# Four edits and a new instruction order in a fused attention, gMLP and expert-attention kernel: a twin copy from PSUM, a normalisation in one product, a minimum as a reduction

## The chip, the core and the metric

The kernel runs on one core of a Trainium2 chip. The metric is the device time of one execution in microseconds (us), as the median over several runs. The engines named below are PE (TensorE, which multiplies matrices), PEld (its weight loads), DVE (VectorE), ACT (ScalarE), POOL (GpSimd) and SP (SyncE, which issues the transfers between HBM and the on-chip memory). SBUF is the on-chip memory. PSUM is the eight banks into which PE writes its results.

## The reference

Three layers follow each other. The inputs are fp32.

```
# 1: attention with a window of 64; 4 batches, 8 heads, 576 positions, head size 64
scores = scale * q @ k^T;  mask: 0 <= i - j < 64
attn = softmax(scores);    x = attn @ v           -> x: (4, 576, 512)
# 2: gated MLP
h = relu(x @ w_in);  u, v = h[:, :512], h[:, 512:]
v_n = (v - mean(v)) / sqrt(var(v) + 1e-6)
x = (u * (w_spatial @ v_n + b_spatial)) @ w_out   -> x: (4, 576, 512)
# 3: four experts, two of them per token, each a causal attention
logits = x @ w_gate;  the two largest per token -> weights w (softmax over the two)
for e in 4 experts:
    q, k, v = x @ wq[e], x @ wk[e], x @ wv[e]
    a = softmax(causal(scale * q @ k^T))
    out += w[:, e] * (a @ v @ wo[e])
```

The products of the second and third layer are computed from fp32 numbers that are split into a high part and a low part, so that most products appear as two or three matmuls.

## The kernel before

A small list scheduler, the class Planner, lays out the program when the kernel is built. Each step is a node with the engines that may run it and a cost on each, the nodes that it waits for, the buffers that it uses, and a priority. The planner goes through the ready nodes, takes for each engine the one that stands best, and writes out the instructions in that order. Nothing of it runs on the chip: what the chip sees is one fixed instruction list for each engine, and semaphores between them. Three dictionaries named SHIFT (one for PE steps, one for the other engines, one for transfers) add a number to the priority of each single node. A few scalars weigh the rest: SWITCH (a change between kinds of matmul), DVE_BIAS and POOL_BIAS (which engine takes a step that several could run), EFT and others. So a new table means a new order on every engine, and a step that may run on several engines may land on another one.

The planner runs twice. The first run holds the first attention (function a_couple), the unpacking of the weights (prep64, lines 674 to 696), and the first product of the gMLP with its statistics and the spatial mix. The second run holds the rest: the projections q and k of the third layer (c_qk), v (c_v, c_vt), the gate (c_gate), the causal attention in units of a row block and an expert (unit), the product with v (c_pv), with wo (c_wo), and the splitting of the layer's input into high and low part (c_split, names xh and xl).

The steps that matter here, by their lines:

- The start. `heat` issues WARM filler matmuls at the very start and FILL = 60 more where PE would have nothing to do. They multiply the identity by itself (L333, `bank<-ident`).
- First attention, in steps of three 128x128 blocks. PE forms the scores (names vt, ut, kt for k and qa for q). DVE adds the mask and takes the row minimum (L546). ACT takes the exponential (L552). DVE sums and inverts (L568, L570). `s_norm` scales the three blocks, each with its own column of factors, on ACT (L558) or on DVE or POOL (L560). PE transposes the result (L564), and it is multiplied by v (`pt,woh`).
- Projection k (c_qk). The product lies in a PSUM bank. `hi` rounds it into kd, one half of the partitions for each of two experts. `lo` subtracts that from the bank (its result is named kz in the trace, L357). `twin` puts a second copy of the high part into the other half of the partitions of kd. In the kernel before it copies kd to kd within SBUF, and waits for `hi`.
- The gate (c_gate, L1155 to L1170) is a chain of some fifteen small DVE instructions, ranks the four logits and leaves the weights in fx.
- A unit: PE forms the scores from kd, kz and qs. DVE adds the causal mask and takes the minimum (L1207). For the last block of rows there are two halves, and L1216 takes the smaller of the two minima. ACT takes the exponential (L1219). DVE adds a small number to the sum and inverts it (L1221, L1222). DVE or POOL scales by the inverse and by fx (L1223), so that this step waits for the gate. PE transposes (L1239), the result is copied to pg, and PE multiplies pg by v (`pg,v`).

Of the kernel before, what the change touches and what calls it, by code (L numbers as in the profile page):

```python
# [26 lines left out]
SWITCH = 107920.0  # L27
A_BIAS = 10098.0
C_BIAS = 162315.0
DVE_BIAS = (1136.0, 1147.0)  # L30
POOL_BIAS = (1131.0, 1068.0)
WARM = 8
FILL = 60
LOADS = (-130000, -120000, -43801, -5807, 14591, 18276, 34028)
EFT = (636.0, 778.0)
# [233 lines left out]
def attn_gmlp_moe_kernel(ctx: ExitStack, tc: tile.TileContext, kq0, qT, kT, v, w_in, wspT, b_sp, w_outT,  # L269
# [6 lines left out]
    HS = S // 2  # L276
# [221 lines left out]
    def a_couple(n0):  # L498
# [25 lines left out]
        def vap(x, vi, e):  # L524
            b, p, _ = grp[x]
            c = e * 64 + (0 if b else (p % 2) * 128)
            return hv[x][:, vi, c:c + 64]

        def s_mm(_):
            for j in range(3):  # L530
                for x, e in ((0, 0), (1, 1), (1, 0), (0, 1)):
                    win = max(0, 64 * (3 * grp[x][2] + j - 1))
                    mm(bank[e][HALF[x], j * 128:(j + 1) * 128], qap(x, j, e), kap(x, win, e))

        def mask(j):
            return MASK[tuple(int(3 * g + j > 0) for _, _, g in grp)]

        S_N[n0] = S_N[n0 + 1] = top = N((PE, 816), s_mm, kn + [Q_N[n0], Q_N[n0 + 1], S_N.get(n0 - 1)], alloc=bank, use=hk, prio=prio,
                                        form=1)
        done = []  # L540
        for ps, pt in zip(bank, pts):
            pa, mx, ps2 = r_pa.new(), r_mx.new(), r_at.new()

            def s_top(_, ps=ps, pa=pa, mx=mx):
                for j in range(3):
                    dve.tensor_tensor_reduce(out=pa[:, j, :], in0=ps[:, j * 128:(j + 1) * 128],  # L546
                                             in1=mask(j), scale=-0.125, scalar=3.0e38,
                                             op0=ALU.add, op1=ALU.min, accum_out=mx[:, j, 0:1])

            def s_exp(_, pa=pa, mx=mx):  # L550
# [4 lines left out]
            def s_norm(e, pa=pa, mx=mx):  # L555
                for j in range(3):
                    if e == ACT:
                        act.activation(pa[:, j, :], pa[:, j, :], AF.Copy, scale=mx[:, j, 3:4])  # L558
                    else:
                        engs[e].tensor_scalar(pa[:, j, :], pa[:, j, :], mx[:, j, 3:4], 1.0, op0=ALU.mult, op1=ALU.mult)  # L560
# [460 lines left out]
    def c_qk(b, pr, h, nm):  # L1021
# [28 lines left out]
        else:  # L1050
# [9 lines left out]

            def twin(e):
                for x in range(2):
                    copy(e, kd[x][HALF[1 - x], tk], kd[x][HALF[x], tk])
            n1 = N(halves(HS), hi, [a], use=[ps] + kl + kd)
            n2 = N((DVE, 2 * t_tt(HS) + 185), lo, [n1], use=[ps] + kl + kd)
            n3 = N(halves(HS, False), twin, [n1], use=kd, sbuf=True)
            a = N({DVE: 0.0}, lambda e: None, [n2, n3])
        QK_N.setdefault((b, pr, nm), []).append(a)

    V2, V2_N, LG_N, FX = {}, {}, {}, {}  # L1070
    VT, VT_N = {}, {}

# [356 lines left out]
```

## Time and profile before

| quantity | value |
|---|---|
| median of 3 runs | 450.18 us (449.14 to 451.76) |
| the profiled execution, its own time | 450.96 us |
| its span, first to last instruction | 449.2 us |
| PE busy | 439.7 us, 98% of the span |
| PEld busy | 397.4 us, 88% |
| DVE busy | 315.9 us, 70% |
| ACT busy | 293.7 us, 65% |
| POOL busy | 105.5 us, 23% |
| chain that ended last, PE's share | 80% (DVE 8%, ACT 6%, DMA 3%) |
| mean granted TensorE clock | 0.996 |

1.76 us of the profiled execution's time lie outside the span. The busy shares are means over stages that differ. The profile gives for any stretch of the span the busy time of each engine, the TensorE clock that was granted (1.00 is 2.4 GHz, half of it 1.2 GHz) and the share of time in which the transfer engines worked. For each engine it gives what ended its idle times. A group of instructions is shown as line, engine, operation and `output<-input`, with the minimum, median and maximum of its durations in ns. Matmul durations overlap, since matmuls are pipelined.

### The profile page before, as it was taken

To read this page: it belongs to the slowest core of one execution; us is meant where nothing else is said; L and a number is where in the kernel's file an instruction comes from. 1 tells how busy PE (TensorE), PEld (TensorE's weight loads), DVE (VectorE), ACT (ScalarE), POOL (GpSimd) and SP (SyncE) were. 2 spreads that over 40 slices of the span, in tenths; PEclk is the share of its full clock that TensorE was granted. 3 is DMA by queue.
4 is the path that set the end of the run, shared out by engine and by line. 5 is a ranking of instruction groups with operands and counts; after the bars stand their busy time and mean duration, and the time that the engine had idled before them with its cause. 6 is when DMAs were issued, how large, how long until landed. Compare 5 with 4: busy or idle time off the path is not lost.

```text
span 449.2 us, 10878 instructions
## 1 busy us (share of the span) xinstructions
PE 439.7 (98%) x3962; PEld 397.4 (88%) x3962; DVE 315.9 (70%) x1291; ACT 293.7 (65%) x926; POOL 105.5 (23%) x168
## 2 busy tenths in 40 slices
PE   8999999999999999999999999899999999999996
PEld 7887899989899879999899999699899979897875
DVE  4999989962866989024535547988697987787650
ACT  4989989562766968213422347887585978777863
POOL 4335763300300225000100341710031011012110
PEclk9999999999999999999999999989999999999999
DMA  8993737040242505003001000000010001000114
GB/s 286 302 312 113 249 109 233 19 139 0 63 148 65 174 4 140 0 1 95 1 1 48 1 0 2 0 2 3 0 48 26 0 2 49 0 1 25 72 50 161
DMA packets 31079, 33.10 MB, mean 74 GB/s; under 512 B 1905, under 2 KB 24689, under 8 KB 31026
## 3 DMA queue, kind: packets, MB, share of 16 engines
q1 hardware_dynamic: 31026, 32.41, 23.1%
q8 instruction: 31, 0.51, 0.5%
q14 instruction: 22, 0.18, 0.1%
HBM read 27.68 MB, written 4.72 MB: 72 GB/s over the span
## 4 chain that ended last, share of the span: by engine, by line
PE 80%; DVE 8%; ACT 6%; DMA 3%; issue 2%; POOL 2%; POOLq 0%; ACTq 0%
PE bank L333 72%; PE bank L1239 5%; DMA y<-in_w_in_dram 3%; PE bank L564 3%; ACT pa L552 1%; DVE p L1207 1%; ACT pa L558 1%; DVE p L1223 1%; ACT p L1219 1%; DVE qs L357 1%; POOL p L1223 1%; DVE xh L348 1%; ACT bank L679 0%; ACT pt L344 0%; DVE kz L357 0%
## 5 line engine op out<-in xcount | busy, mean ns | idle before, releaser
L333 PE MATMUL bank<-xh,w 128*128 128x288 f32 x512 | 109.6, 298 | 0.0
L333 PEld LDWEIGHTS bank<-xh,w 128*128 128x128 f32 x512 | 84.1, 188 | 0.9 <-DVE st L767 0.2
L333 PE MATMUL bank<-xl,w 128*128 128x288 f32 x256 | 75.3, 294 | 0.0
L333 PE MATMUL bank<-w,xh 128*128 128x512 f32 (+1 forms) x256 | 65.1, 344 | 0.0
L552 ACT ACTIVATE pa<-pa,mx 128x128 f32<-128x128 f32 x144 | 55.8, 398 | 5.5 <-DVE mx L546 5.4
L333 PEld LDWEIGHTS bank<-xl,w 128*128 128x128 f32 x256 | 48.2, 188 | 0.4
L333 PEld LDWEIGHTS bank<-w,xh 128*128 128x128 f32 x256 | 43.5, 190 | 5.4 <-ACT pt L344 0.2
L1219 ACT ACTIVATE p<-p,mc 128x128 f32<-128x128 f32 (+4 forms) x72 | 41.8, 582 | 8.6 <-DVE mc L1207 7.1
L1223 POOL TENSOR_SCALAR p<-p,mc,fx 128x256 f32<-128x256 f32 (+4 forms) x26 | 17.1, 661 | 113.9 <-DVE mc L1222 54.8
L333 PE MATMUL bank<-w,xl 128*128 128x512 f32 (+1 forms) x128 | 43.4, 339 | 0.0
L333 PE MATMUL bank<-wsp_h,vh 128*128 128x288 f32 x128 | 38.6, 302 | 0.0
L333 PE MATMUL bank<-wsp_h,vl 128*128 128x288 f32 x128 | 37.7, 295 | 0.0
L333 PE MATMUL bank<-wsp_l,vh 128*128 128x288 f32 x128 | 37.7, 294 | 0.0
L1207 DVE CUSTOM_DVE_ANT_0 p<-bank,cmask 128x128 f32<-128x128 f32 (+4 forms) x72 | 33.2, 482 | 6.1 <-PE bank L333 4.2
L770 POOL TENSOR_TENSOR st<-st,nhalf 128x1 f32<-128x1 f32 (+1 forms) x20 | 11.5, 573 | 98.3 <-DVE st L769 98.3
L1239 PE MATMUL bank<-ident,p 128*128 128x128 f32 x192 | 30.8, 282 | 2.9 <-DVE mc L1221 1.9
L344 ACT ACTIVATE pg<-bank 128x128 f32<-128x128 f32 (+4 forms) x71 | 29.2, 440 | 6.6 <-PE bank L1239 6.0
L546 DVE CUSTOM_DVE_ANT_0 pa<-bank,mask 128x128 f32<-128x128 f32 x120 | 28.3, 284 | 5.2 <-POOL mx L415 4.1
L333 PE MATMUL bank<-kd,qs 128*128 128x128 f32 (+5 forms) x96 | 30.9, 338 | 0.0
L1239 PEld LDWEIGHTS bank<-ident,p 128*128 128x128 f32 x192 | 23.2, 143 | 7.4 <-DVE mc L1221 2.9
L333 PE MATMUL bank<-kz,qs 128*128 128x128 f32 (+5 forms) x96 | 28.7, 316 | 0.0
L552 ACT ACTIVATION_READ_ACCUMULATOR pa<-pa,mx 128x1 f32 x144 | 28.4, 197 | 0.0
(209 smaller groups left out, 1077.0 us busy)
## 6 DMA issues: line engine op xcount, KB each, us to landing
vt<-in_v_dram SPq DMA_DIRECT2D x12, 512.0 KB, 4.5
qa<-in_qT_dram SPq DMA_DIRECT2D x44, 96.0 KB, 3.8
out_dram<-ot SPq DMA_DIRECT2D x15, 256.0 KB, 2.0
y<-in_w_in_dram SPq DMA_DIRECT2D x7, 512.0 KB, 7.2
kt<-in_kT_dram SPq DMA_DIRECT2D x12, 288.0 KB, 4.4
y<-in_w_outT_dram SPq DMA_DIRECT2D x4, 512.0 KB, 4.3
y<-in_wspT_dram SPq DMA_DIRECT2D x2, 576.0 KB, 4.0
vt<-in_kq_dram SPq DMA_DIRECT2D x2, 384.0 KB, 3.8
```

The lines of the kernel that those rows point to most:

```text
L333: pe.matmul(o, lhsT, rhs, start=start, stop=stop)
L344: act.activation(o, i, AF.Copy)
L348: engs[e].tensor_copy(o, i)
L357: engs[e].tensor_tensor(out=o, in0=a, in1=hi.bitcast(F32), op=ALU.subtract)
L546: dve.tensor_tensor_reduce(out=pa[:, j, :], in0=ps[:, j * 128:(j + 1) * 128], in1=mask(j), scale=-0.125, scalar=3.0e38, op0=ALU.add, op1=A ...
L552: act.activation(pa[:, j, :], pa[:, j, :], AF.Exp, bias=mx[:, j, 0:1], scale=-1.0, accum_out=mx[:, j, 1:2])
L564: pe.transpose(ps2[:, j * 128:(j + 1) * 128], pa[:, j, :], ident)
L770: a = N((POOL, 464), lambda e: pool.tensor_tensor(out=st[:m, 9:10], in0=st[:m, 8:9], in1=nhalf[:m], op=ALU.pow), [n1], use=[st])
L1207: dve.tensor_tensor_reduce(out=P[:, a0:a1], in0=ps[:, :w], in1=msk, scale=-0.125, scalar=3.0e38, op0=ALU.add, op1=ALU.min, accum_out=mc[:, ...
L1219: a = N((ACT, 284 + 0.87 * L), lambda e: act.activation(P[:m, :L], P[:m, :L], AF.Exp, bias=mc[:m, 0:1], scale=-1.0, accum_out=mc[:m, 2:3]) ...
L1223: a = N({POOL: 328 + 0.832 * L, DVE: 90 + 0.52 * L}, lambda e: engs[e].tensor_scalar(P[:, :L], P[:, :L], mc[:, 3:4], fx[:, I, ev:ev + 1], ...
L1239: pe.transpose(ps[:, j * m:(j + 1) * m], P[:, j * 128:(j + 1) * 128], ident)
```

## The change

The edits by themselves are small; the three tables and the scalars above replace the whole order.

```
-SWITCH = 107920.0
+SWITCH = 76763.0
-DVE_BIAS = (1136.0, 1147.0)
-POOL_BIAS = (1131.0, 1068.0)
-WARM = 8
+DVE_BIAS = (1180.0, 1793.0)
+POOL_BIAS = (1364.0, 1322.0)
+WARM = 4
-EFT = (636.0, 778.0)
+EFT = (759.0, 1125.0)
 SHIFT = (
...
-        S_N[n0] = S_N[n0 + 1] = top = N((PE, 816), s_mm, kn + [Q_N[n0], Q_N[n0 + 1], S_N.get(n0 - 1)], alloc=bank, use=hk, prio=prio,
+        S_N[n0] = S_N[n0 + 1] = top = N((PE, 816 if n0 else 1500), s_mm, kn + [Q_N[n0], Q_N[n0 + 1], S_N.get(n0 - 1)], alloc=bank, use=hk, prio=prio,
...
             def s_norm(e, pa=pa, mx=mx):
-                for j in range(3):
-                    if e == ACT:
+                if e == ACT:
+                    for j in range(3):
                         act.activation(pa[:, j, :], pa[:, j, :], AF.Copy, scale=mx[:, j, 3:4])
-                    else:
-                        engs[e].tensor_scalar(pa[:, j, :], pa[:, j, :], mx[:, j, 3:4], 1.0, op0=ALU.mult, op1=ALU.mult)
+                else:
+                    engs[e].tensor_tensor(out=pa.t, in0=pa.t, in1=mx[:, :, 3:4].to_broadcast([128, 3, 128]), op=ALU.mult)
...
             def twin(e):
                 for x in range(2):
-                    copy(e, kd[x][HALF[1 - x], tk], kd[x][HALF[x], tk])
+                    copy(e, kd[x][HALF[1 - x], tk], ps[HALF[x], :HS])
...
-            n3 = N(halves(HS, False), twin, [n1], use=kd, sbuf=True)
+            n3 = N(halves(HS), twin, [a], use=[ps] + kl + kd)
...
-        def N_(c, f, deps, alloc=()):
-            return N((DVE, c), lambda e: f(), deps, alloc=alloc, use=[] if alloc else [ex, ga, gb])
+        def N_(c, f, deps, alloc=(), sbuf=True):
+            return N((DVE, c), lambda e: f(), deps, alloc=alloc, use=[] if alloc else [ex, ga, gb], sbuf=sbuf)
...
-            tops = [N((DVE, 70), lambda e: dve.tensor_tensor(out=mc[:m, 0:1], in0=mc[:m, 0:1], in1=mc[:m, 1:2],
-                                                             op=ALU.min), tops, use=[mc], prio=prio)]
+            tops = [N((DVE, 75), lambda e: dve.tensor_reduce(out=mc[:m, 0:1], in_=mc[:m, 0:2], axis=AX.X, op=ALU.min),
+                      tops, use=[mc], prio=prio)]
```

The cost numbers in the nodes (816, 1500, 70, 75 and the like) are the planner's weights, and change only the order. The flag `sbuf` of the gate's steps is such a weight too. Of the gate's instructions none changes.

The PE list goes from 2237 to 2231 rows, the DVE list from 1210 to 1224, ACT from 522 to 516, SP from 74 to 77; POOL keeps 139. Nearly every row of the PE list stands elsewhere. Three places show how.

The first is the head of SP's list, the transfers of the first stage. in_v is read into woh and wol, in_kT into ut and kt, in_qT into qa. Before:

```order
L426 DMA vt<-in_kq_dram 128x768 x2
L426 DMA w_149<-in_w_in_dram 128x1024
L426 DMA woh<-in_v_dram 128x2x256
L426 DMA y_152<-in_w_in_dram 128x1024
L426 DMA y_154<-in_w_in_dram 128x1024
L426 DMA y_156<-in_w_in_dram 128x1024
L426 DMA wol<-in_v_dram 128x2x256
L426 DMA qa<-in_qT_dram 128x192 x2
L426 DMA ut<-in_kT_dram 128x4x256
```

After:

```order
L426 DMA vt<-in_kq_dram 128x768 x2
L426 DMA woh<-in_v_dram 128x2x256
L426 DMA wol<-in_v_dram 128x2x256
L426 DMA w_147<-in_w_in_dram 128x1024
L426 DMA ut<-in_kT_dram 128x4x256
L426 DMA qa<-in_qT_dram 128x192 x2
L426 DMA y_166<-in_w_in_dram 128x1024
L426 DMA ut<-in_kT_dram 128x4x192
L426 DMA y_169<-in_w_in_dram 128x1024
L426 DMA y_178<-in_w_in_dram 128x1024
```

The first piece of k (ut) moves ahead of three of the four pieces of w_in.

The second is DVE where the third layer's attention begins. L1207 is the mask and minimum of a unit, L1221 and L1222 its sum and inverse, L1155 to L1170 the gate, `lg_104` the logits of the first batch. Before, the gate's last rows stand ahead of the first units:

```order
L1169 TENSOR_TENSOR fx<-fx,gb 128x20
L1170 COPY fx<-fx 64x2
L357 TENSOR_TENSOR kz_3625<-bank_70,kd 64x288
L357 TENSOR_TENSOR kz_3626<-bank_70,kd 64x288
L1207 ISA p,mc<-bank_69,cmask 128x128
L1207 ISA mc 128x1
L1207 ISA p,mc<-bank_66,cmask 128x256
L1207 ISA mc 128x1
L1207 ISA p,mc<-bank_71,cmask 128x128
```

After:

```order
L1207 ISA p,mc<-bank_66,cmask 128x256
L1207 ISA mc 128x1
L1221 TENSOR_SCALAR mc<-mc 128x1
L1087 COPY lg_104<-bank_69 128x4
L1222 RECIPROCAL mc<-mc 128x1
L1155 TENSOR_REDUCE gb<-lg_104 128x5
L1221 TENSOR_SCALAR mc<-mc 128x1
L1156 TENSOR_TENSOR ga<-lg_104 128x80
L1222 RECIPROCAL mc<-mc 128x1
```

The whole first gate moves from ahead of the first four units' L1207 to behind them, and the first L1223 of these units stands behind L1170. The third is DVE a little ahead of that place, where the k projections of the first batch are finished. In the kernel before DVE has only the rows `kz` there, and both copies of kd are ACT's. After:

```order
L348 CAST kd<-bank_69 64x288 x2
L357 TENSOR_TENSOR kz_3555<-bank_69,kd 64x288
L357 TENSOR_TENSOR kz_3556<-bank_69,kd 64x288
L357 TENSOR_TENSOR kz_3557<-bank_67,kd 64x288
L357 TENSOR_TENSOR kz_3558<-bank_67,kd 64x288
L1087 COPY lg_104<-bank_68 128x4
L348 CAST kd<-bank_72 64x288 x2
```

A pair `CAST kd<-bank` is a twin that now runs on DVE. 12 of the 16 twins do so after, none before; the other 4 stay on ACT. In the program after, each of the 12 still waits for ACT as well as for PE.

## Rows read from the trace of the kernel before

**Rows 1.** Windows: us, PE, PEld, DVE, ACT, POOL busy (instructions), PEclk, DMA share, GB/s

```profile
6.00:46.00 40.00, 38.62 (x502) 33.23 (x498) 36.61 (x176) 36.42 (x140) 16.99 (x28) 1.00 0.83 264
46.00:280.00 234.00, 234.00 (x2267) 218.08 (x2260) 151.09 (x595) 131.78 (x439) 55.63 (x85) 1.00 0.23 70
...
289.00:293.00 4.00, 2.12 (x17) 1.98 (x16) 4.00 (x14) 1.92 (x5) 1.86 (x2) 0.95 0.00 0
293.00:297.00 4.00, 4.00 (x24) 3.95 (x24) 2.36 (x15) 3.05 (x10) 0.77 (x1) 0.62 0.00 0
...
300.00:446.00 146.00, 144.84 (x1058) 125.67 (x1056) 108.40 (x436) 108.17 (x303) 19.59 (x25) 1.00 0.09 31
```

**Rows 2.** Waits of PE: line, waited for: us in total, times, longest

```profile
PE bank L1239 <- DVE mc L1221: 1.9, 1, 1.9
...
PE bank L1239 <- POOL p L1223: 0.7, 3, 0.3
PE bank L564 <- DVE pa L560: 0.7, 1, 0.7
...
PE bank L1239 <- DVE p L1223: 0.2, 1, 0.2
```

**Rows 3.** Chain that ended last, a piece of it: start, us, what

```profile
30.84 5.00 DMA y<-in_w_in_dram
```

**Rows 4.** Fillers, by form: duration ns minimum/median/maximum, first and last start

```profile
L333 PE MATMUL bank<-ident x136: 272/275/579, 1.6 to 203.0; 128*128 128x128 f32 x136
```

**Rows 5.** s_norm and subtractions with two SBUF operands, by form, same columns

```profile
L560 DVE TENSOR_SCALAR pa<-pa,mx x75: 270/282/1474, 10.6 to 177.6; 128x128 f32<-128x128 f32 x75
...
L357 DVE TENSOR_TENSOR vl<-vr,vh x10: 692/693/695, 99.7 to 224.0; 128x512 fp32r<-128x512 f32 x10
...
L357 DVE TENSOR_TENSOR xl<-pa,xh x5: 459/459/461, 235.1 to 257.6; 128x288 fp32r<-128x288 f32 x5
```

**Rows 6.** Timeline at 22 to 26 us, DVE and POOL: start, us, engine, line

```profile
23.18 1.53 DVE L560 TENSOR_SCALAR pa<-pa,mx 128x128 f32<-128x128 f32 x3
25.16 0.67 DVE L560 TENSOR_SCALAR pa<-pa,mx 128x128 f32<-128x128 f32 x3
...
22.97 1.27 POOL L357 TENSOR_TENSOR w<-y,w 128x512 fp32r<-128x512 f32 x1 [2.82 <-ACT w L344]
```

**Rows 7.** Timeline, 288 to 292 us, DVE, POOL, ACT and PE

```profile
288.09 2.77 POOL L357 TENSOR_TENSOR xl<-y,xh 128x576 fp32r<-128x576 f32 x2
...
288.24 1.27 DVE L1216 TENSOR_TENSOR mc<-mc 128x1 f32<-128x1 f32 x1
...
289.44 1.64 DVE L1223 TENSOR_SCALAR p<-p,mc,fx 128x384 f32<-128x384 f32 x1
289.61 0.78 ACT L1219 ACTIVATE p<-p,mc 128x576 f32<-128x576 f32 x1 [0.66 <-DVE mc L1216]
...
291.14 0.55 PE L1239 MATMUL bank<-ident,p 128*128 128x128 f32 x3 [1.88 <-DVE mc L1221]
```

**Rows 8.** The minimum of two halves, L1216, by form

```profile
L1216 DVE TENSOR_TENSOR mc<-mc x8: 148/158/1274, 288.2 to 420.5; 128x1 f32<-128x1 f32 x8
```

**Rows 9.** Copies of k's high part, by form

```profile
L344 ACT ACTIVATE kd<-kd x32: 428/442/446, 264.7 to 416.2; 64x288 fp32r<-64x288 f32 x32
...
L344 ACT ACTIVATE kd<-bank x30: 388/406/408, 264.0 to 415.4; 64x288 fp32r<-64x288 f32 x30
L348 DVE CAST kd<-bank x2: 450/455/460, 301.0 to 301.5; 64x288 fp32r<-64x288 f32 x2
```

**Rows 10.** First and last instruction of a gate, from DVE's timeline

```profile
309.04 0.18 DVE L1155 TENSOR_REDUCE gb<-lg 128x5 f32<-128x20 f32 x1
...
312.33 0.17 DVE L1170 COPY fx<-fx 64x2 f32<-64x2 f32 x1
```

**Rows 11.** The mask of a unit and its exponential, by form

```profile
L1207 DVE CUSTOM_DVE_ANT_0 p<-bank,cmask x72: 273/452/692, 279.9 to 429.6; 128x128 f32<-128x128 f32 x16, 128x256 f32<-128x256 f32 x16, 128x384 f32<-128x384 f32 x16, 128x512 f32<-128x512 f32 x16
...
L1219 ACT ACTIVATE p<-p,mc x72: 387/604/779, 280.3 to 431.3; 128x128 f32<-128x128 f32 x16, 128x256 f32<-128x256 f32 x16, 128x384 f32<-128x384 f32 x16, 128x512 f32<-128x512 f32 x16
```

More of the change, by code (lines that the diff above doesn't have):

```diff
@@ L570, in a_couple @@
             a = N((DVE, 91), lambda e, mx=mx: dve.reciprocal(mx[:, :, 3], mx[:, :, 3]), [a], use=[mx], prio=prio)
-            a = N({POOL: 1053, DVE: 450, ACT: 880}, s_norm, [a], use=[pa, mx], prio=prio, sbuf=True)
+            a = N({POOL: 955, DVE: 468, ACT: 880}, s_norm, [a], use=[pa, mx], prio=prio, sbuf=True)
             a = N((PE, 327), p_t, [a], alloc=[ps2, pt], use=[pa], prio=prio)
@@ L1149, in lead @@
             return m1(n)[:, :, None].to_broadcast(s3)
-        def N_(c, f, deps, alloc=()):
-            return N((DVE, c), lambda e: f(), deps, alloc=alloc, use=[] if alloc else [ex, ga, gb])
+        def N_(c, f, deps, alloc=(), sbuf=True):
+            return N((DVE, c), lambda e: f(), deps, alloc=alloc, use=[] if alloc else [ex, ga, gb], sbuf=sbuf)
         tt, tr_ = dve.tensor_tensor, dve.tensor_reduce
-        n1 = N_(90, lambda: tr_(out=m1(0), in_=lg, axis=AX.X, op=ALU.max), LG_N[b], [ex, ga, gb])
+        n1 = N_(90, lambda: tr_(out=m1(0), in_=lg, axis=AX.X, op=ALU.max), LG_N[b], [ex, ga, gb], False)
         n2 = N_(155, lambda: tt(out=gt(), in0=lf, in1=le, op=ALU.is_gt), [n1])
@@ L1160, in c_gate @@
         n4 = N((ACT, 210), lambda e: act.activation(ex.t, ex.t, AF.Exp), [n4], use=[ex])
-        nf = N_(0, lambda: None, [n2, n3, n4])
+        nf = N_(0, lambda: None, [n2, n3, n4], sbuf=False)
         n2 = N_(155, lambda: tt(out=gt(), in0=gt(), in1=eq(), op=ALU.add), [n2, n3])
-        n2 = N_(150, lambda: tr_(out=rk(), in_=gt(), axis=AX.X, op=ALU.add), [n2])
+        n2 = N_(150, lambda: tr_(out=rk(), in_=gt(), axis=AX.X, op=ALU.add), [n2], sbuf=False)
         n2 = N_(80, lambda: dve.tensor_scalar(rk(), rk(), 1.5, None, op0=ALU.is_lt), [n2])
         n2 = N_(90, lambda: tt(out=ex.t, in0=ex.t, in1=rk(), op=ALU.mult), [n2, n4])
-        n2 = N_(90, lambda: tr_(out=m1(1), in_=ex.t, axis=AX.X, op=ALU.add), [n2])
+        n2 = N_(90, lambda: tr_(out=m1(1), in_=ex.t, axis=AX.X, op=ALU.add), [n2], sbuf=False)
         n2 = N_(70, lambda: dve.tensor_scalar(m1(1), m1(1), 1e-9, None, op0=ALU.add), [n2])
-        n2 = N_(75, lambda: dve.reciprocal(m1(1), m1(1)), [n2])
+        n2 = N_(75, lambda: dve.reciprocal(m1(1), m1(1)), [n2], sbuf=False)
         n4 = N_(90, lambda: tt(out=ex.t, in0=ex.t, in1=lead(1), op=ALU.mult), [n2])
```

6 rows, old and new, of the table SHIFT are left out of this document.

## The prediction, made before the changed kernel was timed

> **What bounds the kernel now.** I read the stretches of the span first, then what PE waited for, then the timeline at the one long wait. The windows [rows 1] show four stages with different limits. From 6 to 46 us PE is busy for 38.62 of 40 us, but 64 of the 68 fillers (136 instructions) lie before 44 us and give the next stage nothing [rows 4]. DVE is busy for 36.61 us there and ACT for 36.42: the first stage is set by the chain mask, exponential, sum, scaling, and by DVE above all. From 46 to 280 us PE is busy for 234.00 of 234.00 us. There a shorter step on another engine buys nothing, and only a new hole in PE can cost. From 280 to about 297 us the attention of the third layer starts, and PE has its only long hole: 1.88 us, all of it behind one DVE instruction [rows 2, 7]. Right behind it the granted clock falls to a mean of 0.95 in 289 to 293 us and 0.62 in 293 to 297 us [rows 1], that is, to its lower level for a few microseconds. From 300 us to the end of the matmuls PE is busy for 144.84 of 146 us, with DVE at 108.40 and ACT at 108.17, about 74% each. Its waits there are short, all on the scaling L1223: 0.7 us in three places and 0.2 us in one, 0.2 us each [rows 2].
>
> So what can be won is small: fillers and holes ahead of 46 us, the 1.88 us with the clock behind it, and some 1 us later on. What can be lost is open on the other side, since the order is new throughout.
>
> **Yardstick.** The profiled execution took 450.96 us, 0.78 above the median of 450.18. Each term below is a difference to that execution, and the sum is taken off the median, as the terms don't depend on the 0.78. 0.5% is 2.25 us, about what a measurement of this kernel can tell from no change; faster begins at 447.93, slower at 452.43.
>
> **Edit 1, the product in s_norm.** Three scalings on DVE take 0.67 us as a group where nothing disturbs, and 1.53 us where POOL runs a subtraction of two SBUF operands beside it [rows 6]. One product over 384 columns lies between 0.46 us (288 columns) and 0.69 us (512 columns) [rows 5], by a straight line 0.56 us: 0.11 us less a group. There were 25 such groups (75 instructions), and some ten ahead of 46 us, so about 1.1 us less for DVE in the stage that it sets, from 0 to 2 by the ends. The groups behind 46 us lie beside a full PE and give nothing. POOL's seven groups I cost at nothing for the same reason; were one late, PE would wait for its transposes, as it did once for DVE, 0.7 us [rows 2].
>
> The 1.53 us stand beside a POOL subtraction, and the 0.67 us two microseconds later do not [rows 6]. The Trainium skill, "SBUF — State Buffer", § Who interferes with whom, says of this that scalings which use both ports and products with two SBUF operands alike share a port with POOL, one of the two blocking for a whole instruction. By that rule the one product loses as much to POOL as the three scalings, and the sum keeps 0.11 us a group and not more; the rows of the scalings agree, and no row here shows a product beside POOL.
>
> **Edit 2, L1216.** The minimum of two columns took 0.15 us mostly and 1.27 us once, beside POOL's two subtractions of 2.77 us [rows 7, 8]. The exponential behind it began 0.66 us late. The next DVE instruction, an L1223, was stretched to 1.64 us by the same neighbour, and L1221 came behind that: that queue is the 1.88 us of PE. As a reduction over one operand, the step lies between 0.15 us (L1216 undisturbed) and 0.18 us (L1155, the gate's reduction) [rows 8, 10] if POOL does not hold it, and at 1.27 us if it does. I take 0.18. Alone this would free about 1.1 us of the 1.88, as the stretched L1223 stays what it is. The 1.27 us row lies wholly within POOL's 2.77 us. The same page of the Trainium skill says that on this chip a reduction never blocks against POOL, so by it the step stays short wherever the new order puts it; no row here shows a reduction of mc beside POOL.
>
> **Edit 3, the twin.** A copy from SBUF takes ACT 442 ns, from PSUM 406 ns, and DVE from PSUM 455 ns [rows 9]. It would start without waiting for `hi`, but the program after makes each of the 12 twins on DVE wait for ACT too, which reads the same bank. So what was 0.81 us (hi, two copies) and then 0.92 us of `lo` on DVE beside 0.88 us of twin on ACT, 1.7 us, becomes 0.81, 0.91 and 0.92 one behind the other, 2.6 us. That is 0.9 us later for 12 of 16 steps, hidden where k is ready well ahead of its scores. And DVE gets 12 x 0.91 = 10.9 us more to do and ACT 12 x 0.88 = 10.6 us less, most of it behind 300 us, where DVE goes from 74% to about 81%. I take it into the last term below.
>
> **The order, stage by stage.** *To 46 us.* WARM 8 to 4 takes four fillers off; at the start the clock is low and they stand ahead of nothing that is late, so this is worth nothing by itself to some 0.9 us if PE's queue is what is late. k's first piece moves ahead of three pieces of w_in. In the kernel before, the chain ran through w_in's transfers, 5.00 us in one piece [rows 3], so w_in later can cost, and k earlier can help. Laying the DVE work out in either order up to the same first-attention step gives nearly the same amount before (32 us) and after, less the 1.1 us of edit 1. I take a gain of **1.3 us**, range -0.7 to 2.2.
>
> *46 to 280 us.* PE is full; in the new order at least 5.5 us of PE work lie between a score product and its transposes (at least 6.1 before). **0**, down to -0.5.
>
> *280 to 297 us.* Before: 1.88 us of hole, 0.27 us of small ones and some 0.5 us of smaller lateness, 2.7 us; and the clock, (1 - 0.62) x 4 + (1 - 0.95) x 4 = 1.7 us [rows 1]. Together 4.4. After: the gate stands behind the first four L1207, and the first L1223 behind the gate. A gate took 3.5 us from first to last instruction [rows 10], of which 1.1 us went to other work between; so 2.4 us. With four masks (1.5 us) and eight small instructions of 0.15 us, 5.3 us pass on DVE between the first mask and the first scaling, and 0.34 us of scaling (128 columns, the least of L1223) follow. PE has ten units of scores in a row and a projection behind them, 4.9 us, ahead of the first transpose. So PE waits there about 0.8 us, then 0.4 us for the copy ahead of `pg,v`, and 0.2 to 1.1 us where the v products want their split input: 2.3 us, range 1.2 to 3.5. No single hole reaches 1.88 us, and I expect the clock to stay. Gain 4.4 - 2.3 = **2.1 us**, range 0.9 to 3.2.
>
> *300 us to the end.* I laid the matmuls of either order end to end at the durations of their groups and read how much PE work lies between a unit's last score product and its first transpose. The unit needs L1207 (0.45 us), L1219 (0.60) with its sum, L1221, L1222 and L1223, with hand-overs 2.2 to 3.4 us [rows 11]. Before, 4 units of 80 had under 2.8 us, and four waits of 0.2 us stand in the trace [rows 2]. After, 11 units have under 2.8, four of them in one burst. 7 more x 0.2 = **1.4 us lost**, range from a gain of 0.5 to a loss of 3.0, the upper end if DVE's added 10.9 us fall on these units. The last matmul and the output transfer stay as they are.
>
> Sum: 1.3 + 0 + 2.1 - 1.4 = 2.0 us less. 450.18 - 2.0 = **448.2 us**.
>
> **Rivals.**
> 1. *The last term does not appear.* ACT is relieved by 10.6 us and L1216 is no longer stretched, so the short units get their exponential sooner. For it: ACT was as busy as DVE. Against it: DVE takes what ACT loses. The gate may also be hidden. Time: 448.2 - 1.4 - 1.2 = 445.6. Chance 0.20.
> 2. *The gate is late enough to bring the clock down again.* The holes at 280 us add up in one place, as with the 1.88 us before. For it: it fell once, behind one such hole [rows 1, 7]. Against: mine are spread over three places. Time: 448.2 + 1.7 = 449.9. Chance 0.17.
> 3. *The start gives nothing*, because w_in's later transfer holds DVE as it did [rows 3]. Time: 448.2 + 1.3 = 449.5. Chance 0.12.
> 4. *The change does not do what it says of the twin*: k is later by 0.9 us. Were 4 of the 12 not hidden, 3.6 us: 448.2 + 3.6 = 451.8. Against: before, PE shows no wait for kd or kz. Chance 0.05.
> 5. *Slower.* DVE becomes the bound behind 300 us: twins, a gate and masks queue ahead of a scaling, PE has a hole of the kind at 289 us, and the clock falls again: 1.88 + 1.7 = 3.6 us each. One such hole with rival 2 gives 450.18 - 1.3 - 0.4 + 1.4 + 3.6 = 453.5. It decides from a DVE queue of about 2 us more than the unit's cover. Chance 0.10.
>
> **How the numbers follow.** The forecast has 0.36, with its own range of 446.2 to 450.3 by the terms' ends. A little under half of it is faster by over 0.5%. Faster: 0.45 x 0.36 + 0.20 + a little of 2 and 3 = 0.40. Slower: rival 5, half of 4, and the forecast's tail: 0.15. Same: 0.45. The range reaches from rival 1 to just past the start of slower, 445.0 to 452.2, leaving out most of rival 5 and the faster half of a better rival 1.
>
> **What would show it.** The first product over kt should end its wait 1 to 1.5 us sooner (edit 1 and the start). No hole over 1.5 us at 280 to 297 us, and the clock at 1.00 there; if the clock falls, rival 2. L1216 never over 0.3 us. DVE about 81% busy behind 300 us, with some ten waits of 0.2 us on L1223; fewer speak for rival 1, one of 2 us for rival 5. A wait of PE for kd or kz would show rival 4. The prediction is wrong if PE is no longer full between 46 and 280 us, or if one of the new waits lies where nothing of before showed one.

## Result and profile after the change

The changed kernel took 453.51 us in the median of five runs (452.73 to 454.01), against 450.18 before: 1.0067 times as long, 95% interval 1.0045 to 1.0089. The forecast was 448.2, in a range of 445.0 to 452.2, so it was wrong in size and in sign. The profiled execution took 452.73 us, 1.77 more than the profiled one of before, with a span of 450.9 us and a granted clock of 1.00 throughout. The other four executions had means of 0.995 to 0.999. The profiled one of before had paid 1.7 us for its clock, so like for like the distance is about 3.5 us, against 3.3 us by the medians.

The windows after, with the columns of [rows 1]:

```profile
6.00:46.00 40.00, 39.22 (x508) 33.97 (x506) 37.13 (x166) 36.09 (x136) 17.52 (x24) 1.00 0.84 270
46.00:280.00 234.00, 233.59 (x2239) 217.39 (x2240) 150.45 (x572) 133.30 (x433) 51.15 (x70) 1.00 0.23 69
280.00:289.00 9.00, 7.42 (x54) 6.17 (x53) 7.94 (x41) 6.08 (x20) 4.96 (x6) 1.00 0.00 1
...
293.00:297.00 4.00, 3.27 (x26) 2.91 (x26) 3.32 (x15) 2.62 (x10) 0.77 (x1) 1.00 0.02 4
...
300.00:446.00 146.00, 142.30 (x1037) 122.48 (x1036) 109.55 (x444) 101.76 (x291) 20.23 (x26) 1.00 0.08 28
```

PE stays full from 46 to 280 us but for 0.41 us, the end of a hole that began at 45.7 us. Its idle time from 300 to 446 us went from 1.16 [rows 1] to 3.70 us. Of the 1.16 us of before, 0.36 lie behind the last matmul, so the stretch behind 300 us lost some 2.9 us. The waits of PE after, as in [rows 2]:

```profile
PE bank L1239 <- POOL p L1223: 1.9, 3, 1.1
...
PE bank L1239 <- DVE p L1223: 1.1, 3, 0.7
PE bank L333 <- ACT pg L344: 0.7, 1, 0.7
...
PE bank L1239 <- DVE lg L1087: 0.6, 1, 0.6
PE bank L1239 <- DVE mc L1221: 0.6, 1, 0.6
PE bank L1239 <- DVE pg L348: 0.5, 1, 0.5
```

The one hole of 1.9 us is gone, and many of 0.5 to 1.1 us have come. In none of them does PE wait for kd or kz. DVE's own waits tell more. First the kernel before, then the changed one:

```profile
DVE kz L357 <- ACT kd L344: 4.8, 3, 2.1
```

```profile
DVE kd L348 <- ACT kd L344: 13.2, 11, 2.2
...
DVE kz L357 <- ACT kd L344: 1.1, 2, 0.6
```

DVE stood still for ACT's first copy of k for 4.8 us in 3 places before, and for 14.3 us in 13 places after. Here is what that does at the longest hole, from the timeline of the changed kernel:

```profile
298.15 0.19 ACT L1219 ACTIVATION_READ_ACCUMULATOR p<-p,mc 128x1 f32 x1
...
298.24 0.81 ACT L344 ACTIVATE kd<-bank 64x288 fp32r<-64x288 f32 x2
...
299.09 0.92 DVE L348 CAST kd<-bank 64x288 fp32r<-64x288 f32 x2 [0.77 <-ACT kd L344]
...
299.94 0.14 DVE L1221 TENSOR_SCALAR mc<-mc 128x1 f32<-128x1 f32 x1
300.11 0.92 DVE L357 TENSOR_TENSOR kz<-bank,kd 64x288 fp32r<-64x288 f32 x2
301.06 0.16 DVE L1087 COPY lg<-bank 128x4 f32<-128x4 f32 x1
301.26 0.17 DVE L1222 RECIPROCAL mc<-mc 128x1 f32<-128x1 f32 x1
...
301.59 0.55 POOL L1223 TENSOR_SCALAR p<-p,mc,fx 128x256 f32<-128x256 f32 x1 [2.62 <-DVE mc L1222]
...
302.20 0.44 PE L1239 MATMUL bank<-ident,p 128*128 128x128 f32 x2 [1.07 <-POOL p L1223]
```

The twin waits 0.77 us for ACT and takes 0.92, kz takes 0.92 behind it, and the reciprocal of a unit whose sum of exponentials was there at 298.34 us stands in DVE's queue behind both, at 301.26. POOL waits for that, and PE for POOL: 1.07 us.

### The profile page after: what moved, and what is told of

Same layout as the page of the kernel before. It is cut to its first block, busy times and chain, and to the rows that moved or that the text cites. A ratio compares the mean times of both kernels' runs of the same rounds, so it can differ in the third digit from the quotient of the medians.

```text
span 450.9 us, 10833 instructions
## 1 busy us (share of the span) xinstructions
PE 438.6 (97%) x3954; PEld 394.6 (88%) x3954; DVE 315.9 (70%) x1264; ACT 289.1 (64%) x908; POOL 102.0 (23%) x149
## 4 chain that ended last, share of the span: by engine, by line
PE 80%; DVE 9%; ACT 7%; issue 1%; POOL 1%; ACTq 0%; POOLq 0%; DVEq 0%
PE bank L333 73%; PE bank L1239 4%; PE bank L564 3%; ACT p L1219 2%; DVE p L1207 2%; ACT pa L552 1%; DVE kz L357 1%; DVE kd L348 1%; ACT kd L344 1%; ACT xh L344 1%; ACT pg L344 1%; DVE xl L357 1%; DVE p L1223 1%; DVE pa L546 1%; ACT pt L344 0%
## 5 line engine op out<-in xcount | busy, mean ns | idle before, releaser
L1223 POOL TENSOR_SCALAR p<-p,mc,fx 128x256 f32<-128x256 f32 (+4 forms) x27 | 18.7, 692 | 129.5 <-ACT p L1219 34.1
L1207 DVE CUSTOM_DVE_ANT_0 p<-bank,cmask 128x128 f32<-128x128 f32 (+3 forms) x72 | 33.3, 483 | 5.4 <-PE bank L333 4.4
L344 ACT ACTIVATE pg<-bank 128x512 f32<-128x512 f32 (+4 forms) x79 | 31.9, 435 | 3.1 <-PE bank L1239 2.3
L1239 PEld LDWEIGHTS bank<-ident,p 128*128 128x128 f32 x192 | 22.1, 140 | 10.5 <-POOL p L1223 4.1
L333 PE MATMUL bank<-kd,qs 128*128 128x288 f32 (+5 forms) x96 | 30.1, 330 | 0.0
L344 ACT ACTIVATE pt<-bank 128x384 f32<-128x384 f32 x42 | 19.0, 491 | 15.9 <-PE bank L564 15.8
L835 DVE TENSOR_TENSOR y<-bank,ut 128x288 f32<-128x288 f32 x24 | 10.9, 456 | 25.5 <-PE bank L333 25.5
```

The lines of the kernel that those rows point to most:

```text
L333: pe.matmul(o, lhsT, rhs, start=start, stop=stop)
L344: act.activation(o, i, AF.Copy)
L835: dve.tensor_tensor(out=o, in0=ps[:, :HS], in1=u[:, d, tk], op=ALU.mult)
L1207: dve.tensor_tensor_reduce(out=P[:, a0:a1], in0=ps[:, :w], in1=msk, scale=-0.125, scalar=3.0e38, op0=ALU.add, op1=ALU.min, accum_out=mc[:, ...
L1223: a = N({POOL: 328 + 0.832 * L, DVE: 90 + 0.52 * L}, lambda e: engs[e].tensor_scalar(P[:, :L], P[:, :L], mc[:, 3:4], fx[:, I, ev:ev + 1], ...
L1239: pe.transpose(ps[:, j * m:(j + 1) * m], P[:, j * 128:(j + 1) * 128], ident)
```

## Experiments

Where an order is said to be held, every engine's instruction list is that of the kernel named, and only the instructions shown differ. The theories: A, the twins harm because they stand on DVE; B, the gate behind the first masks; C, the new order as such; D, the twin's length and its wait, on whichever engine (D2: because it reads the bank); E and F part what is left between order and twin. "Before" was run again beside each set, with medians of 449.5 to 450.0 us; ratios are to those runs.

**The twin alone, in the order of before.** The twin's source is the one line; in the second kernel 12 of the 16 twins are DVE's besides.

```
-                    copy(e, kd[x][HALF[1 - x], tk], kd[x][HALF[x], tk])
+                    copy(e, kd[x][HALF[1 - x], tk], ps[HALF[x], :HS])
```

> The kernel before with its order held; only the twin's source is changed, from kd in SBUF to the bank, all 16 on ScalarE as before. Theory D2: kz starts behind the twin, 0.8 us later in 16 places, new holes at about 307, 364 and 408 us, 451 to 452.5 us. Rival C: a copy from the bank is 36 ns shorter and needs no wait, 449.3 to 450.2 us.

Measured: 452.98 us, ratio 1.0078 (1.0055 to 1.0101). This one line, on the same engine and in the old order, costs as much as the whole change, and half a microsecond more than theory D2 allowed. The first k projection in the trace, the kernel before and then this one:

```profile
264.00 0.83 ACT L344 ACTIVATE kd<-bank 64x288 fp32r<-64x288 f32 x2 [1.20 <-PE bank L333]
264.74 0.90 ACT L344 ACTIVATE kd<-kd 64x288 fp32r<-64x288 f32 x2
264.87 0.92 DVE L357 TENSOR_TENSOR kz<-bank,kd 64x288 fp32r<-64x288 f32 x2 [0.87 <-ACT kd L344]
```

```profile
263.77 1.65 ACT L344 ACTIVATE kd<-bank 64x288 fp32r<-64x288 f32 x4 [1.20 <-PE bank L333]
265.45 0.92 DVE L357 TENSOR_TENSOR kz<-bank,kd 64x288 fp32r<-64x288 f32 x2 [1.69 <-ACT kd L344]
```

From SBUF the twin ran beside kz. From the bank, kz starts only when the twin has ended, and DVE waits 1.69 in place of 0.87 us. Over the whole run:

```profile
DVE kz L357 <- ACT kd L344: 13.4, 10, 2.9
```

against 4.8 us in 3 places before. PE's waits for units grew with it, against 1.9 us on L1221 in one place and 0.7 us on POOL in three before [rows 2]:

```profile
PE bank L1239 <- DVE mc L1221: 2.8, 3, 1.8
PE bank L1239 <- POOL p L1223: 1.6, 5, 0.7
...
PE bank L1239 <- ACT qs L344: 0.5, 1, 0.5
```

Behind 300 us PE's holes come to 2.9 us, against 0.8 us before, and the three longest, of 0.74, 0.50 and 0.54 us, begin at 307, 364 and 408 us, the places that theory D2 had named. PE itself waits only once behind a copy of k, 0.2 us.

The Trainium skill, "PSUM — Partial Sum Buffer", § PSUM bank collisions raise a hardware error, says that two engines must not be in one bank and quadrant at a time, and that nothing in the hardware makes one wait, so the program has to keep them apart. The trace agrees in so far as kz waits for ACT's copy and the two never overlap in these rows; what an overlap would do, no run here shows.

> The kernel before with its order held; the twin copies read PSUM, and the same 12 of 16 are issued on VectorE at the place where ScalarE did them. This is the one part alone, in the old order. Theory A: a hold of VectorE of some 0.9 us and a wait for ScalarE in front of units makes PE holes here too, 1.5 to 3.5 us, so 451.7 to 453.7 us. Theories B and C: not more than 0.7 us above 450.2.

Measured: 455.64 us, ratio 1.0127 (1.0109 to 1.0144), more than any theory gave. In this profile PE shows five waits on POOL's L1223 of 3.2 us together, and two on L1221 of 2.2. The first stage, in which nothing differs, was 1.7 us later than in the profile of before; some of the ratio may be that. But behind 300 us too PE's holes come to 4.6 us, against 2.9 with the twins on ACT, and DVE is busy for 118.34 of 146 us there, 81%. So in this order it counts as well which engine takes the twins.

**The twin in the new order.** Three kernels: the 12 twins given to ACT; all 16 given to ACT and read from SBUF again (the line above undone); none at all. In the last one `hi` writes all 128 partitions of the bank at once, so the other half of kd holds another expert's numbers:

```
             def hi(e):
                 for x in range(2):
-                    copy(e, kd[x][HALF[x], tk], ps[HALF[x], :HS])
+                    copy(e, kd[x][:, tk], ps[:, :HS])
...
-                    copy(e, kd[x][HALF[1 - x], tk], ps[HALF[x], :HS])
+                    pass
```

> The changed kernel with its whole order held instruction by instruction, except that the 12 twin copies of k that stood on VectorE are issued on ScalarE at the same place, right behind the first copy of the same bank. Theory A (the twins on VectorE: each waits there for ScalarE's first copy, 13.2 us of VectorE standing still in 11 places, and then takes 0.91 us, with a unit's scaling queued behind): the holes at 294, 295 and 301 us, 2.4 us together, shrink by most, so 450.5 to 451.5 us. Theory B (the gate behind the first four masks makes the loss): nothing here touches that, 453 to 454 us. Theory C (the new order as a whole leaves units too short a cover): within 0.7 us of 453.5. Against all: ScalarE gets 10.6 us more and the exponentials come later, then slower than 454.

Measured: 452.87 us, ratio 1.0085 (1.006 to 1.0109), no gain. My theory A, that the twins are harmful because they stand on DVE, fell here for the changed order: DVE now waits for ACT's copies before kz, 19.2 us in 13 places.

> The changed kernel with its order held; only the twin is undone: all 16 twin copies are ScalarE's again and read kd in SBUF, not the bank. Theory D2 (the twin from the bank makes the subtraction kz wait until the twin is done, on whichever engine it is, since both read the same bank; from SBUF the two run side by side): most of the 3.9 us that leaving the twins out gave comes back, 449.5 to 451 us. Rival C (the order is slow by itself, the twin's work and not its wait counts): 452 to 453.5 us, as with the twin from the bank on ScalarE.

Measured: 451.47 us, ratio 1.0035 (1.0020 to 1.0051). The time lies between the ranges of theories D2 and C. The hole before the transposes at 302 us shrank, DVE's wait for kd went from 19.2 to 10.9 us. About half of the loss comes back. ACT's list has the 12 copies at places where the planner had laid them on DVE.

> The changed kernel with its order held and without its 16 twin copies: the first copy takes all 128 partitions of the bank in the same time, so that the other half of kd holds numbers of the other expert. Theory D (the new order takes the twin for a step beside the first copy, the chip does one after the other, and the 0.9 us hold either engine, whichever takes it, with units queued behind): 449.5 to 451 us, and the holes at 294 and 301 us are gone. Theory C in its plain form (short covers and buffers elsewhere): 452 to 453.5 us.

Measured: 449.17 us, ratio 0.9986 (0.9966 to 1.0006). Without twins the changed kernel loses nothing against the kernel before. Two rows of waits, of DVE and of PE:

```profile
DVE kz L357 <- ACT kd L344: 10.5, 12, 1.9
```

```profile
PE bank L1239 <- POOL p L1223: 0.6, 1, 0.6
```

PE's holes behind 300 us come to 1.0 us, against 3.7 us in the changed kernel, and this one of 0.60 us is the only one over 0.2 us. Yet DVE still stands for ACT's first copy of k almost as long as with the twins from SBUF, 10.5 against 10.9 us. So the sum of these waits does not set the loss, and what the twin from SBUF costs in this order stays open.

**The gate.** The first batch's gate is left out, in the new order, but for one copy:

```
-            return N((DVE, c), lambda e: f(), deps, alloc=alloc, use=[] if alloc else [ex, ga, gb], sbuf=sbuf)
+            return N((DVE, c), lambda e: f() if b else alloc and dve.tensor_copy(ex.t, lg), deps, alloc=alloc, use=[] if alloc else [ex, ga, gb], sbuf=sbuf)
...
-        n4 = N((ACT, 210), lambda e: act.activation(ex.t, ex.t, AF.Exp), [n4], use=[ex])
+        n4 = N((ACT, 210), lambda e: b and act.activation(ex.t, ex.t, AF.Exp), [n4], use=[ex])
```

> The changed kernel with its order held, without the first batch's gate: one small copy stands in the place of its VectorE instructions, and its one ScalarE instruction is left out, so the weights of the first batch are not computed. Theory B: the transposes at 283 to 286 us no longer wait, 2.2 us of holes there go to 0.5 or less, so 451.5 to 452 us. Theory A: the holes at 294 to 301 us stay, and what is won at 283 us is lost there again in part, 452.5 to 453.5 us. Theory C: within 0.7 us of 453.5.

Measured: 453.29 us, ratio 1.0083 (1.0069 to 1.0096), no gain. Theory B fell. The timeline shows why:

```profile
282.20 0.65 DVE L1223 TENSOR_SCALAR p<-p,mc,fx 128x128 f32<-128x128 f32 x2
284.31 0.27 PE L1239 MATMUL bank<-ident,p 128*128 128x128 f32 x1
284.62 0.29 DVE L348 COPY pg<-bank 128x128 f32<-128x128 f32 x1 [1.77 <-PE bank L1239]
285.06 0.30 PE L1239 MATMUL bank<-ident,p 128*128 128x128 f32 x1 [0.47 <-DVE pg L348]
...
286.98 0.44 PE L333 MATMUL bank<-pg,v 128*64 128x256 f32 x2 [0.75 <-ACT pg L344]
```

The scalings are done 1.5 us ahead of the transposes, which PE's list has behind a projection. The holes stay, 0.47 and 0.75 us: a transpose waits until the copy has emptied its bank, and the product with v follows the copies with nothing between.

**The other edits, in the order of before.**

> The kernel before with its order held; only the minimum of the two halves is a reduction over one operand. If the lock by GpSimd made the 1.88 us hole: L1216 goes from 1.27 to about 0.15 us, the hole to 0.8 us, and the clock behind it does not fall, 447.3 to 449.1 us. Rival: the scaling L1223 behind it (1.64 us) meets GpSimd all the same and is held from then on, the hole stays near 1.9 us and the clock falls, 449.5 to 450.5 us.

Measured: 448.54 us, ratio 0.9978 (0.9965 to 0.9991): 0.2% faster. The same stretch as in [rows 7]:

```profile
288.10 2.90 POOL L357 TENSOR_TENSOR xl<-y,xh 128x576 fp32r<-128x576 f32 x2
...
288.25 0.13 DVE L1216 TENSOR_REDUCE mc<-mc 128x1 f32<-128x2 f32 x1
288.36 1.37 DVE L1223 TENSOR_SCALAR p<-p,mc,fx 128x384 f32<-128x384 f32 x1
...
289.78 0.55 PE L1239 MATMUL bank<-ident,p 128*128 128x128 f32 x3 [0.52 <-DVE mc L1221]
```

The reduction takes 0.13 us beside POOL's two subtractions, where the minimum over two operands took 1.27. The scaling behind it is still stretched. The hole is 0.52 in place of 1.88 us, and the clock was granted at 1.00 through this stretch.

> The kernel before with its order held; only s_norm on VectorE and GpSimd is one product instead of three scalings. As predicted: 0.11 us less a group on the stage that VectorE sets, 448.7 to 449.7 us. Rival: the broadcast factor or GpSimd's lock makes the product slower than the three scalings, 450 to 451 us.

Measured: 449.45 us, ratio 1.0001 (0.9980 to 1.0021): nothing that can be measured, though DVE was busy for 34.52 us from 6 to 46 us in place of 36.61 [rows 1].

> All edits to the instructions (product in s_norm, twin from PSUM on ScalarE, minimum as a reduction) in the whole order of before, held, with 8 warm fillers. Theory C: the edits are worth what the reduction alone was, or a little more, 447.5 to 449 us. Rival (an edit costs by itself): 450 us or more.

Measured: 450.83 us, ratio 1.0018 (1.0004 to 1.0031), slower than expected by theory C and as its rival had it: an edit costs by itself. The reduction at 0.9978, the product at 1.0001 and the twin at 1.0078 would multiply to 1.0057; the 0.4% between is about what the intervals allow. The gain of the reduction is eaten by the twin.

**The two runs of the planner apart.**

> The reverse: all edits, the first run in the order of before, the second run in the changed order. Theory C: as slow as the changed kernel or up to 1.5 us slower, 452.5 to 454.5 us. Rival: 451 us or less.

Measured: 453.28 us, ratio 1.0073 (1.0050 to 1.0096), as slow as the changed kernel. The order of the first run makes no difference that can be measured.

> The changed kernel's code with all its edits; the planner's first run (first attention to the spatial mix) in the changed order, its second run (the projections and the second attention) in the order of before, held instruction by instruction, all twin copies on ScalarE as in that order. Theory C (the second run's order makes the whole loss): the start's gain of about 1 us stays and the reduction's gain is added, 446.5 to 448.5 us. Rival (the loss comes from the first run or from the edits themselves): 450 us or more.

Measured: 451.16 us, ratio 1.0032 (1.0015 to 1.0048). This is in the rival's range, not in that of theory C: the edits lose by themselves in the old order of the second run. But it is half of the loss of the changed kernel; the rest came with the new order of the second run.

> All edits but the twin's (which reads SBUF on ScalarE as before), the first run in the changed order, the second in that of before. Theory D2: the reduction's gain without the twin's loss, 447.5 to 449 us, the fastest of all. Rival C and any loss from the product: 450 us or more.

Measured: 448.06 us, ratio 0.9962 (0.9950 to 0.9974). This is the fastest of all, and beats both kernels.

> All edits, the first run in the changed order, the second in that of before, and no twin copies at all: the first copy takes all 128 partitions of the bank in the same time, as in after_twin_free. With after_twin_free (449.2 us) this compares the two orders of the second run with the twin's time and waits taken out of both. Theory E (the new order loses for itself, by short covers and by transposes, copies and products in direct succession at 283 to 286 us): 446 to 447.7 us, 1.5 us or more under after_twin_free. Theory F (the new order loses only through the twin, whose length it was not laid out for): 448.5 to 449.7 us.

Measured: 448.51 us, ratio 0.9963 (0.9949 to 0.9976). In the old order of the second run, twins from SBUF cost nothing: 0.9962 with, 0.9963 without. In the new order they cost 0.5% even on ACT and from SBUF (1.0035 against 0.9986). The two orders without any twin lie 0.23% apart, and their intervals overlap, so whether the new order loses by itself, some 1 us or nothing, stays open. What is shown is the twin's share: taking it out of the changed kernel brings 0.8%, more than the whole loss.

All with the start of the changed kernel, ratios to before:

| second run's order | twin from the bank | twin from SBUF, on ACT | no twin |
|---|---|---|---|
| of before | 1.0032 | 0.9962 | 0.9963 |
| changed | 1.0067 (12 on DVE), 1.0085 (on ACT) | 1.0035 | 0.9986 |

## Why the prediction was wrong, point by point

**The twin (edit 3) is the step that failed.** I read from the program that the twin waits for ACT, worked out 2.6 us for 1.7, and then took the 0.9 us as hidden, since "k is ready well ahead of its scores". That is so, and in the changed kernel PE never waits for k. But the wait is DVE's, and the sum did not price what is queued behind it: masks, sums and inverses of units that are due. The runs show that line alone at 1.0078 in the old order, some 3.5 us. I also took it for a matter of the 12 twins on DVE; it holds for ACT's as well, since kz reads the bank too. Rival 4 stood on the right wait and had 0.05, at 451.8 us, because I asked for a PE wait on kd, and none came in the changed kernel. Rival 5, with 0.10, had 453.5 us, the time that was measured, and a queue of twins ahead of a scaling. But it asked for one hole of 1.88 us with the clock behind it. The longest behind 300 us was 1.07 us, one of several, and the clock of that execution stayed at 1.00. That its number was met is luck.

**280 to 297 us, gain 2.1 forecast.** The holes by the windows are 1.58 + 0.73 = 2.3 us, the size forecast, against 2.15 by the same rows before. The places were not. The gate gave some 0.2 us (1.58 us of holes from 280 to 289 us with it, 1.39 without), where I had 0.8; the parts that I named for it add up to 5.1 us and not to 5.3, which would have left 0.5. Copies between transposes and products gave the larger part. The clock stayed at 1.00 in the profiled execution, as forecast, but three of the five executions had a mean of 0.995 or 0.996, so rival 2 is not excluded. The failure is in the base: 1.7 us for the clock were taken from one execution and subtracted from the median of all, though the clock falls in some executions of either kernel. Of the 83 executions of the kernel before beside the experiments 23 had a mean of 0.995 or 0.996, with a median of 450.7 us, against 449.5 us for the others. So the median holds little of the 1.7 us.

**300 us to the end, loss 1.4 forecast, 2.9 measured.** Waits of units behind a fuller DVE queue came, as forecast, but the term was mis-sized, and what fills it is another. I took 0.2 us for each of seven short units, 1.4 us. The same order without twins has only 0.2 us more of holes there than the kernel before, so some 2.7 of the 2.9 us came with the twins. Four holes had 0.6 to 1.1 us: ahead of the transposes at 302, 387 and 419 us a twin or kz stood in DVE's queue, and the one at 325 us is there without twins too. DVE did not go to 81% busy: 109.55 of 146 us is 75%. So it was not the sum of DVE's work that rose, but what stood in front of due units.

**The start, gain 1.3.** Not shown: the first product over kt, forecast 1 to 1.5 us sooner, began at 34.24 us in place of 34.44. With the first run's order exchanged the ratio was 1.0073 against 1.0067, and two profiles whose first stages hold the same instructions lie up to 1.7 us apart there.

**Edit 2** was right: the step took 0.13 us beside POOL's subtractions in the kernel with that edit alone. In the changed kernel it takes 0.15 us, but none of the eight stands beside a POOL subtraction there.

```profile
L1216 DVE TENSOR_REDUCE mc<-mc x8: 145/151/156, 290.2 to 422.6; 128x1 f32<-128x2 f32 x8
```

Alone it is worth about 1 us, as much as forecast; what it wins in the changed order no run shows. **Edit 1** was right in the length of the product, and no gain in time was measured: it has the interpolated 0.56 us and is held by POOL like the scalings, 1.58 us beside a subtraction. In the trace of before 7 of the 25 groups lie ahead of 46 us, not some ten, and DVE's 2.1 us less in that stage brought nothing that can be measured, so DVE's busy time alone does not set the stage.

```profile
L560 DVE TENSOR_TENSOR pa<-pa,mx x27: 547/559/1576, 9.1 to 193.3; 128x384 f32<-128x384 f32 x27
```

**46 to 280 us** was right, 0.4 us of idle time in 234.

## What to carry to other kernels

Before a copy is pointed at PSUM to save it a wait, see which other engine reads that bank: the copy then shares the bank with it, and one of the two stands in front of everything queued behind it. Where a step waits on an engine that works in order, price the queue behind it and not only the step's own consumer; the sum of such waits is no price, since 10.5 us of them cost nothing here without twins. A clock that fell in one profiled execution belongs to that execution, and a gain from it is not to be taken off a median.

## What the hardware showed that was not expected

The granted clock did not follow the size of the hole. Behind PE's hole of 1.88 us the mean was 0.62 in the profile of before [rows 1, 2]. In the kernel with only the twin from the bank the same place had 1.8 us, and the clock stayed:

```profile
289.00:293.00 4.00, 2.16 (x18) 2.02 (x18) 4.00 (x12) 1.74 (x5) 2.02 (x2) 1.00 0.00 0
293.00:297.00 4.00, 4.00 (x35) 4.00 (x35) 3.61 (x21) 3.96 (x14) 0.77 (x1) 1.00 0.02 4
```

In the changed order without twins it fell, behind holes of 0.75 us at most, while the changed kernel has holes of 0.47 and 0.75 us in the same place and kept 1.00:

```profile
280.00:289.00 9.00, 7.43 (x44) 5.78 (x43) 7.46 (x40) 5.65 (x21) 4.27 (x5) 0.85 0.00 1
289.00:293.00 4.00, 4.00 (x32) 4.00 (x32) 3.79 (x17) 3.00 (x8) 3.63 (x3) 0.90 0.00 0
```

What decides it in an execution, these runs do not tell.
